# Row ends with places and loads of their own, splits behind the states and queries scaled on GpSimd, in a retention and expert kernel

## Chip, core and metric

One core of a Trainium2 chip (trn2). The metric is device time in microseconds (us) of one execution, from start to end; a kernel's time is the median of its runs, lower is better.

## What is computed

The reference chains three layers, all in float32. Only the first is touched here.

```python
# 1. retention: 4 batches, 8 heads, 576 positions, head size 64
scores = scale * q @ k.T
Dmat = where(rel >= 0, gamma[h] ** rel, 0)      # rel = pos_i - pos_j
ret = (scores * Dmat) @ v
# 2. dense layer on the 2304 tokens, 512 -> 2048 -> 512
h = x @ w_in;  x = (h * sigmoid(1.702 * h)) @ w_out
# 3. each token to one of 8 experts, 512 -> 1024 -> 512, scaled by its gate
out = gate_w * (relu(x @ w1[e]) @ w2[e])
```

## The kernel before

**Stages.** Attention (the retention) comes first, then the dense layer in six blocks of 384 tokens, then the experts. Each engine runs its own list of instructions in the order in which the program writes them; an engine that waits at one instruction holds back all behind it. Loads are issued by SP, also in order.

**Attention.** The work is cut into 16 rows (called `bp` in the code): a row is one batch and one pair of heads, four rows to a batch, so rows 0 to 3 are batch 0, 8 to 11 batch 2. A row's 576 positions are four chunks of 128 and an end of 64. Its chunks are 1 MB (`att`), loaded into one of eight buffers (`NBUF`); the buffer of row n is that of row n-8, and its load waits until that row's last use. The ends of a batch's four rows come in one load of 384 KB (`tails`). Two places hold them, so the ends of batches 2 and 3 take the places of batches 0 and 1 and are loaded when the last `ends_out` of those has run (line 417).

For a row, `decay` multiplies the keys by a table; `scores` makes k-by-q products of the four chunks in two PSUM banks; `masks` multiplies them by the table of decays on VectorE; `state` adds keys times values up chunk by chunk, and ScalarE copies each of the four partial sums out (line 324); `carried` multiplies the queries with these states; `chunk` adds the masked scores times values; `scores_end` and `ends_out` do the same for the ends. `keep` (VectorE) multiplies the result of 512 columns by the queries' decay and takes it out of PSUM, `keep_end` that of the end. For batches 0 and 1 `keep` then splits the result into a high part (ScalarE, line 378) and a low part (GpSimd, line 379) for the dense layer's first two blocks, or copies it (line 381); for batches 2 and 3 it goes straight to a buffer that is written to DRAM later.

The rows run in nine groups: [0], [1, 2], [3, 4] and so on to [13, 14], [15]; group k below is the k-th, from 0. In the loop over groups the current group's rows are `rows`, the next group's `nxt`, and the one after it `then`: `decay` of `then`, `scores_end` of `nxt`, `carried` and `ends_out` of `rows`, `scores` and `masks` of the first of `nxt`, and `values`, which alternates the states of `nxt` with the chunks of `rows`. Behind `values` the loads of rows bp+8 are issued; then come `scores` and `masks` of the second of `nxt`.

**Conversion beside it.** The dense weights come as 16 units of 64-bit words (`wd`, 1 MB each) that ScalarE and VectorE turn into float32 pairs (`convert`): for a unit the magnitude (ScalarE, line 166), two short VectorE steps (lines 179 and 181), two long ones (186, 193), the high part (ScalarE, 169) and the low part (VectorE, 173). `pull(us)` writes as many of these steps as its budget pays for at the place where it is called: in attention at each of the four `yield`s of a group from the third group on, with 0.5 us each. The first three units' loads go out at rows 8, 10 and 13 (`WD_AT`). A unit takes a buffer that attention has done with.

**Dense layer.** For blocks 0 and 1 the steps alternate over the units: `layer1` (12 matmuls into `h`), `swish` (ScalarE, then VectorE into `g..t`, ScalarE `g..h`, a `pull`, VectorE `g..l`), and two steps later `layer2` (9 matmuls into `o`), which needs `g..h` and `g..l`.

## Time and profile before

| | |
|---|---|
| runs, us | 742.16, 743.00, 743.25 (median 743.0) |
| the profiled execution's own time | 742.36 us |
| its span, first to last instruction | 740.6 us |
| TensorE busy | 707.4 us (96%) |
| VectorE, ScalarE, GpSimd busy | 456.2, 305.5, 195.3 us |
| mean granted TensorE clock | 0.988 |
| chain that ended last | TensorE 79%, DMA 13%, VectorE 3% |
| attention's matmuls | 5.7 to 95.8 us |

The profile is one execution, with times from its first instruction. "Busy" counts only the time in which an engine's instructions run; a wait is given with the work that ended it. TensorE (PE) is the busiest engine by far, but the share is a mean over the three stages, and the stage that is changed is the first 13% of the span.

### The profile page before, as it was taken

How to read it: one execution, taken by the hardware profiler on the slowest of the kernel's cores; microseconds unless marked ns; L12 is line 12 of the kernel's file. 1: busy time of each engine (PE TensorE's matmuls, PEld its weight loads, DVE VectorE, ACT ScalarE, POOL GpSimd, SP SyncE). 2: the span in 40 equal slices, each digit the busy share in tenths (PEclk: the TensorE clock that was granted, in tenths of full speed). 3: DMA queues.
4: the chain of work that ended last, by engine and by line, in shares of the span. 5: the costliest groups of instructions: out<-in, count | busy, mean ns of one | idle time of the engine just before them, and what ended most of it. 6: DMA issues, size and time to landing. Idle time of an engine off the chain costs nothing.

```text
span 740.6 us, 13083 instructions
## 1 busy us (share of the span) xinstructions
PE 707.4 (96%) x4882; PEld 654.6 (88%) x4882; DVE 456.2 (62%) x1045; ACT 305.5 (41%) x586; POOL 195.3 (26%) x186
## 2 busy tenths in 40 slices
PE   7875999999999999999999999999999999999995
PEld 6664789898999989899899898989999999999994
DVE  3553798988723887676367548747554654664661
ACT  3332444544427423332233233344345455455542
POOL 1632000000000023030102101224236456566563
PEclk9988999999999999999999999999999999999998
DMA  9955699900021004020210131152778789799861
GB/s 362 419 215 202 215 404 324 310 1 1 29 103 43 2 0 130 1 86 0 82 48 1 43 101 58 59 166 52 217 208 266 214 240 273 210 265 273 250 195 60
DMA packets 52579, 113.40 MB, mean 153 GB/s; under 512 B 8082, under 2 KB 28690, under 8 KB 48288
## 3 DMA queue, kind: packets, MB, share of 16 engines
q1 hardware_dynamic: 49168, 102.55, 43.4%
q0 software_dynamic: 3200, 9.46, 3.6%
q8 instruction: 39, 0.64, 0.3%
q10 hardware_dynamic: 144, 0.52, 0.2%
q14 instruction: 28, 0.23, 0.1%
HBM read 84.67 MB, written 28.17 MB: 152 GB/s over the span
## 4 chain that ended last, share of the span: by engine, by line
PE 79%; DMA 13%; DVE 3%; issue 3%; ACT 1%; POOL 1%; SPq 1%; POOLq 0%; ACTq 0%; DVEq 0%
PE o L501 27%; PE h L490 26%; PE eh L490 10%; PE eo L511 9%; DMA out<-y,idx 7%; DMA ends<-tails 4%; PE ao L332 1%; PE sc L292 1%; PE ao L349 1%; DMA we<-we 1%; PE s L323 1%; DMA row<-att 1%; PE tp L1007 1%; DVE ca L186 0%; DVE unit L173 0%
## 5 line engine op out<-in xcount | busy, mean ns | idle before, releaser
L490 PE MATMUL h<-x,unit 128*128 128x384 f32 x1152 | 217.6, 337 | 0.3 <-DVE g0t L523 0.3
L490 PEld LDWEIGHTS h<-x,unit 128*128 128x128 f32 x1152 | 204.6, 188 | 8.9 <-DVE g0t L523 0.6
L219 POOL TENSOR_TENSOR unit<-we,unit 128x512 fp32r<-128x512 f32 x64 | 102.5, 1609 | 118.2 <-ACT unit L217 107.1
L490 PE MATMUL eh<-xt,unit 128*128 128x336 f32 (+6 forms) x672 | 101.9, 300 | 0.0
L490 PEld LDWEIGHTS eh<-xt,unit 128*128 128x128 f32 x672 | 95.4, 188 | 0.4 <-ACT xt L731 0.2
L218 DVE TENSOR_TENSOR unit<-we,unit 128x512 fp32r<-128x512 f32 x64 | 56.3, 880 | 56.4 <-ACT unit L217 56.4
L597 DVE CUSTOM_DVE_ANT_0 dj<-xr,en 128x512 bf16<-128x512 f32 x120 | 78.0, 696 | 0.0
L217 ACT CAST unit<-we 128x1024 fp32r<-128x1024 f32 x64 | 66.8, 1046 | 23.0 <-DMA we<-we 21.3
L563 POOL TENSOR_TENSOR enrm<-scr,c 128x8 f32<-128x8 f32 x1 | 1.7, 1687 | 164.6 <-ACT ej L568 164.6
L324 ACT ACTIVATE ends<-s,tb 128x64 f32<-128x64 f32 x64 | 19.4, 312 | 47.2 <-PE s L323 46.5
L540 POOL DMA_INDIRECT out<-y,idx x24 | 24.8, 1032 | 30.1 <-ACT y L763 19.6
L540 POOL DMA_INDIRECT xs<-xr,slot x18 | 19.4, 1077 | 39.1 <-DVE xr L672 35.7
L323 PE MATMUL s<-row 128*64 128x64 f32 x256 | 20.2, 235 | 7.3 <-ACT ends L324 6.9
L323 PEld LDWEIGHTS s<-row 128*64 128x64 f32 x256 | 13.4, 135 | 13.6 <-ACT ends L324 12.2
L657 POOL TENSOR_TENSOR cum<-cum,oh_all 128x8 bf16<-128x8 bf16 x18 | 4.8, 265 | 67.2 <-PE rk L650 52.4
L314 POOL TENSOR_TENSOR row<-row,tb 128x512 f32<-128x512 f32 x14 | 14.5, 1044 | 28.5 <-DMA row<-att 28.5
L173 DVE TENSOR_TENSOR unit<-ca,unit 128x1024 fp32r<-128x1024 f32 x16 | 19.5, 1219 | 2.4 <-ACT unit L169 2.4
L292 PE MATMUL sc<-row 64*128 64x128 f32 x256 | 19.6, 294 | 0.8 <-DMA row<-att 0.8
L166 ACT ACTIVATE ca<-wd 128x1024 f32<-128x1024 f32 x16 | 18.4, 1147 | 4.8 <-DVE unit L173 4.8
L186 DVE SCALAR_TENSOR_TENSOR ca<-wd,ca 128x1024 int32<-128x1024 int32 x16 | 19.6, 1222 | 0.3
L193 DVE SCALAR_TENSOR_TENSOR ca<-wd,ca 128x1024 int32<-128x1024 int32 x16 | 19.5, 1217 | 0.0
L292 PEld LDWEIGHTS sc<-row 64*128 64x128 f32 x256 | 16.6, 197 | 2.9 <-issue 1.2
(1302 smaller groups left out, 1514.9 us busy)
## 6 DMA issues: line engine op xcount, KB each, us to landing
we<-we SPq DMA_DIRECT2D x64, 512.0 KB, 4.1
wd<-wd SPq DMA_DIRECT2D x16, 1024.0 KB, 11.9
row<-att SPq DMA_DIRECT2D x15, 1024.0 KB, 9.8
xs<-fill SPq DMA_DIRECT2D x22, 257.0 KB, 10.9
xrow<-xr SPq DMA_DIRECT2D x18, 257.0 KB, 4.0
y<-yd SPq DMA_DIRECT2D x7, 512.0 KB, 4.3
x0d<-x0f SPq DMA_DIRECT2D x4, 768.0 KB, 10.1
x0s<-x0d SPq DMA_DIRECT2D x8, 384.0 KB, 6.5
```

Of the source, the lines that this page charges most:

```text
L173: DVE.tensor_tensor(units[u][:, 1, :], word(u).bitcast(F32), units[u][:, 0, :].bitcast(F32), ALU.subtract)
L186: DVE.scalar_tensor_tensor(a, d[:, :, 1], -0x40000000, a, ALU.bitwise_and, ALU.bitwise_or)
L217: ACT.copy(w[:, 0, :], t)
L218: DVE.tensor_tensor(w[:, 1, :512], t[:, :512], w[:, 0, :512].bitcast(F32), ALU.subtract)
L219: POOL.tensor_tensor(w[:, 1, 512:], t[:, 512:], w[:, 0, 512:].bitcast(F32), ALU.subtract)
L292: PE.matmul(scs[j][:, P * ch : P * (ch + 1)], t[r, P * ch : P * (ch + 1)], t[r, AQ + P * ch : AQ + P * (ch + 1)], start=True, stop=True)
L323: PE.matmul(s[r], t[:, AK + c0 : AK + c0 + 64], t[:, AV + c0 : AV + c0 + 64], start=ch == 0, stop=True, skip_group_check=ch > 0)
L490: PE.matmul(h, w[:, a, P * dc : P * (dc + 1)], xt[:, b, dc, :n], start=k == 0, stop=k == len(terms) - 1)
L501: PE.matmul(o, a[:, c0 : c0 + n], w[:, b, 512:], start=first and k == 0, stop=last and k == 2)
L511: PE.matmul(o, w[:, b, D + P * d : D + P * (d + 1)], a, start=first and k == 0, stop=last and k == 2)
L540: i = POOL.indirect_dma_start(out=dst[:, :], out_offset=bass.IndirectOffsetOnAxis(ap=rows, axis=0), in_=src, in_offset=None, bounds_check= ...
L597: DVE.tensor_tensor_reduce(junk, r[:, :D], en[e // 4][:, e % 4, :], 1.0, 0.0, ALU.mult, ALU.add, dots[:, E * k + e : E * k + e + 1])
```

## The change

- **Ends.** A second buffer (`more`) gives each batch's ends a place of their own. They are loaded right in front of the batch's first row; the load at line 417 is gone. In exchange attention has six row buffers in place of eight (`NBUF`), and the loads of the first three weight units go out at rows 7, 9 and 11. Row 2 is loaded in two halves, keys and values first.
- **Order.** `scores_end` of the next group stands behind `ends_out` of this one.
- **Splits.** What `keep` did behind its multiplication is now `kept_out`, which stands behind all of `values`: ScalarE's splits and copies come after the eight states.
- **Queries.** For batches 2 and 3 GpSimd multiplies the queries by their decay when it decays the keys (128x512 each), and the queries of the ends of a batch (128x256) with its first row; ScalarE then copies the results out of PSUM, and VectorE has nothing to do in `keep` and `keep_end`. Row 1's keys are decayed by GpSimd, too.
- **Pulls.** Two `yield`s to a group, from group 3 on, with a budget of 0.8 us each in group 3 and 1.6 us after it.

```diff
-WD_AT = (8, 10, 13)
+WD_AT = (7, 9, 11)
-NBUF, NROW = 8, 6
+NBUF, NROW = 6, 5
...
-        ends = slot("ends")
-        tl = [ends[:, NPAIR * TAW * i : NPAIR * TAW * (i + 1)].rearrange("p (n w) -> p n w", w=TAW) for i in range(2)]
+        ends, more = slot("ends"), slot("more")
+        tl = [t[:, NPAIR * TAW * i : NPAIR * TAW * (i + 1)].rearrange("p (n w) -> p n w", w=TAW) for t in (ends, more) for i in range(2)]
...
         def load(bp):
             t = row[bp % NBUF]
-            if bp:
+            b, pair = divmod(bp, NPAIR)
+            if bp and pair == 0:
+                SP.dma_start(tl[b], tails[b])
+            if bp == 2:
+                SP.dma_start(t[:, AK:], att[bp, :, AK:])
+                SP.dma_start(t[:, :AK], att[bp, :, :AK])
+            elif bp:
                 SP.dma_start(t, att[bp])
...
-            if bp == 4:
-                SP.dma_start(tl[1], tails[1])
...
         def decay(bp):
...
-                (POOL if bp > 1 else DVE).tensor_tensor(kd, kd, dec.unsqueeze(2).to_broadcast(kd.shape), ALU.mult)
+                (POOL if bp else DVE).tensor_tensor(kd, kd, dec.unsqueeze(2).to_broadcast(kd.shape), ALU.mult)
+                b, pair = divmod(bp, NPAIR)
+                if b > 1:
+                    qd = row[bp % NBUF][:, AQ:AK].rearrange("p (c q) -> p c q", q=P)
+                    POOL.tensor_tensor(qd, qd, tbs[:, pair, :P].unsqueeze(1).to_broadcast(qd.shape), ALU.mult)
+                    if pair == 0:
+                        qe = tl[b][:, :, TQ:TV]
+                        POOL.tensor_tensor(qe, qe, tbs[:, :, :TAIL], ALU.mult)
...
         def keep_end(bp):
-            x = kept_in(bp)[:, NCH * P :]
-            DVE.tensor_tensor(x, st.pop(("ot", bp)), tbs[:, bp % NPAIR, :TAIL], ALU.mult)
+            x, o = kept_in(bp)[:, NCH * P :], st.pop(("ot", bp))
+            if bp // NPAIR > 1:
+                ACT.copy(x, o)
+            else:
+                DVE.tensor_tensor(x, o, tbs[:, bp % NPAIR, :TAIL], ALU.mult)
 
         def keep(bp):
+            if bp // NPAIR > 1:
+                return
...
+        def kept_out(bp):
             b, pair = divmod(bp, NPAIR)
...
             if b > 1:
+                ACT.copy(x[:, : NCH * P], o)
                 return
...
-            scores_end(nxt)
             for bp in rows:
                 carried(bp)
             ends_out(rows)
+            scores_end(nxt)
             for bp in rows:
                 keep_end(bp)
-                b, pair = divmod(bp, NPAIR)
-                if pair == NPAIR - 1 and b + 2 < B:
-                    SP.dma_start(tl[b], tails[b + 2])
-            yield
             if nxt:
                 scores(nxt[0])
                 masks(nxt[0])
-            yield
             values(rows, nxt)
             for bp in rows:
+                kept_out(bp)
...
-            yield
+            yield k
             for bp in nxt[1:]:
                 scores(bp)
                 masks(bp)
-            yield
+            yield k
...
-    for i, _ in enumerate(attention()):
-        if i >= 12:
+    for k in attention():
+        if k > 2:
             flush()
-            pull(0.5)
+            pull(0.8 if k == 3 else 1.6)
```

Three places show how the engines' lists move. A row of them gives the line, the operation, the tile written and those read (with the buffer's number) and the size; lines differ by some 4 to 16 between the two kernels. No time is in them.

SP's list from the fourth row's load on (`row5` is a row buffer, `ends` and `more` the ends' buffers, `wd0` a weight unit). Before:

```order
L258 DMA row4_84<-att 128x2048
L267 DMA ends_90<-tails 128x768
L258 DMA row5_85<-att 128x2048
L258 DMA row6_86<-att 128x2048
L258 DMA row7_87<-att 128x2048
L258 DMA row0_80<-att 128x2048
L136 DMA wd0_272<-wd 128x2048
L258 DMA row1_81<-att 128x2048
L258 DMA row2_82<-att 128x2048
L136 DMA wd1_383<-wd 128x2048
L417 DMA ends_90<-tails 128x768
```

and now:

```order
L259 DMA ends_88<-tails 128x768
L264 DMA row4_84<-att 128x2048
L264 DMA row5_85<-att 128x2048
L264 DMA row0_80<-att 128x2048
L264 DMA row1_81<-att 128x2048
L136 DMA wd0_374<-wd 128x2048
L259 DMA more_89<-tails 128x768
L264 DMA row2_82<-att 128x2048
L264 DMA row3_83<-att 128x2048
L136 DMA wd1_488<-wd 128x2048
```

The ends of batch 1 stand ahead of row 4 and those of batch 2 ahead of row 8 (now in `row2`); before, those of batch 2 stood behind row 10 (`row2`) and the second weight unit.

ScalarE in `values` of group 3, rows 5 and 6, with the states of rows 7 and 8 (`s7`, `s8`), the splits and copies of `x5` and `x6` and a magnitude (`ca`). Before:

```order
L324 ACTIVATE ends_90<-s7_554,tb_88 128x64
L324 ACTIVATE ends_90<-s8_560,tb_88 128x64
L378 CAST x0_1_96<-x5_535 128x192
L381 COPY x0f1_92<-x5_535 128x384
L324 ACTIVATE ends_90<-s7_554,tb_88 128x64
L324 ACTIVATE ends_90<-s8_560,tb_88 128x64
L324 ACTIVATE ends_90<-s7_554,tb_88 128x64
L324 ACTIVATE ends_90<-s8_560,tb_88 128x64
L378 CAST x0_1_96<-x6_537 128x192
L381 COPY x0f2_93<-x6_537 128x384
L166 ACTIVATE ca1_540<-wd1_383 128x1024
```

and now:

```order
L335 ACTIVATE ends_88<-s7_551,tb_86 128x64
L335 ACTIVATE ends_88<-s8_557,tb_86 128x64
L398 CAST x0_1_95<-x5_537 128x192
L401 COPY x0f1_91<-x5_537 128x384
L398 CAST x0_1_95<-x6_539 128x192
L401 COPY x0f2_92<-x6_539 128x384
L166 ACTIVATE ca0_606<-wd0_374 128x1024
L374 COPY x0f0_90<-at7_641 128x64
```

VectorE over the same rows: the first unit's short steps (`ca0`), masks (`sc0`, `sc1`) and `keep` (`x5`, `x6`). Before:

```order
L179 TENSOR_SCALAR ca0_539<-ca0_539 128x1024
L308 SCALAR_TENSOR_TENSOR pr_89<-sc0_102,tb_88 128x512
L308 SCALAR_TENSOR_TENSOR pr_89<-sc1_103,tb_88 128x512
L181 TENSOR_SCALAR ca0_539<-ca0_539 128x1024
L368 TENSOR_TENSOR x5_535<-ao5_512,tb_88 128x512
L368 TENSOR_TENSOR x6_537<-ao6_519,tb_88 128x512
L186 SCALAR_TENSOR_TENSOR ca0_539<-wd0_272,ca0_539 128x1024
L308 SCALAR_TENSOR_TENSOR tb_88<-sc0_102,tb_88 128x512
```

and now:

```order
L383 TENSOR_TENSOR x6_539<-ao6_515,tb_86 128x512
L179 TENSOR_SCALAR ca0_606<-ca0_606 128x1024
L181 TENSOR_SCALAR ca0_606<-ca0_606 128x1024
L312 SCALAR_TENSOR_TENSOR tb_86<-sc0_101,tb_86 128x512
L312 SCALAR_TENSOR_TENSOR tb_86<-sc1_102,tb_86 128x512
L186 SCALAR_TENSOR_TENSOR ca0_606<-wd0_374,ca0_606 128x1024
```

No split stands between two states any more; the first magnitude comes behind both rows' splits, and both short steps that need it stand ahead of the masks of row 8 (the last `sc0`, `sc1` of each list).

VectorE at the dense layer's start, from the end of attention to the first two results of `swish` (`g0t`, `g0l`). Before:

```order
L443 CAST ub_68<-uf_716 128x128
L193 SCALAR_TENSOR_TENSOR ca0_539<-wd2_605,ca0_539 128x1024
L179 TENSOR_SCALAR ca_1020<-ca_1020 128x1024
L523 SCALAR_TENSOR_TENSOR g0t_1054<-g0t_1054,h0_1041 128x384
L181 TENSOR_SCALAR ca_1020<-ca_1020 128x1024
L186 SCALAR_TENSOR_TENSOR ca_1020<-wd3_718,ca_1020 128x1024
L173 TENSOR_TENSOR unit2_1060<-ca0_539,unit2_1060 128x1024
L528 TENSOR_TENSOR g0l_1056<-g0t_1054,g0h_1055 128x384
```

and now:

```order
L181 TENSOR_SCALAR ca_1017<-ca_1017 128x1024
L186 SCALAR_TENSOR_TENSOR ca_1017<-wd3_827,ca_1017 128x1024
L173 TENSOR_TENSOR unit2_1023<-ca0_606,unit2_1023 128x1024
L193 SCALAR_TENSOR_TENSOR ca_1017<-wd3_827,ca_1017 128x1024
L459 CAST ub_68<-uf_825 128x128
L179 TENSOR_SCALAR ca_1017<-ca_1017 128x1024
L181 TENSOR_SCALAR ca_1017<-ca_1017 128x1024
L539 SCALAR_TENSOR_TENSOR g0t_1077<-g0t_1077,h0_1064 128x384
L186 SCALAR_TENSOR_TENSOR ca_1017<-wd4_844,ca_1017 128x1024
L173 TENSOR_TENSOR unit3_1057<-ca_1017,unit3_1057 128x1024
L193 SCALAR_TENSOR_TENSOR ca_1017<-wd4_844,ca_1017 128x1024
L544 TENSOR_TENSOR g0l_1079<-g0t_1077,g0h_1078 128x384
```

All of unit 3 (`wd3`) and the two short steps of unit 4 now stand ahead of `g0t`, and three long steps, not two and a short one, between `g0t` and `g0l`.

## Rows read from the trace of the kernel before

**Rows 1.** The page, granted TensorE clock in 40 slices of the span, in tenths.

```profile
PEclk9988999999999999999999999999999999999998
```

**Rows 2.** Stretches (us): length, busy PE, PEld, DVE, ACT, POOL, clock, DMA share, GB/s.

```profile
17.90:95.84 77.94, 59.39 (x1010) 51.09 (x1008) 43.83 (x82) 27.37 (x74) 21.85 (x26) 0.91 0.70 270
95.84:104.05 8.21, 7.05 (x40) 6.35 (x38) 8.18 (x12) 2.35 (x4) 0.00 (x0) 1.00 1.00 396
104.05:700.00 595.95, 595.29 (x3383) 554.54 (x3384) 382.43 (x916) 253.88 (x466) 151.64 (x137) 1.00 0.43 129
```

**Rows 3.** The chain of waits in time, attention: start us, us, what.

```profile
30.68 10.33 DMA ends<-tails
41.06 0.48 PE sct L298 x4
...
61.66 7.39 DMA ends<-tails
```

**Rows 4.** Waits in attention: engine, line, releaser: us in total, times, longest.

```profile
PE sct L298 <- DMA ends<-tails: 12.3, 3, 7.0
...
PE s L323 <- ACT ends L324: 6.9, 8, 1.7
```

**Rows 5.** Stretches of groups 5 and 6 without a wait, columns as in rows 2.

```profile
74.29:77.54 3.25, 3.25 (x66) 2.54 (x65) 2.10 (x3) 2.24 (x8) 0.00 (x0) 1.00 0.19 33
77.54:78.63 1.09, 1.09 (x18) 0.97 (x16) 0.97 (x2) 0.27 (x1) 0.00 (x0) 1.00 0.77 308
78.63:80.79 2.16, 2.16 (x51) 2.09 (x49) 2.16 (x4) 0.00 (x0) 0.00 (x0) 1.00 0.97 379
```

**Rows 6.** GpSimd's timeline: decays of rows 5 and 6 (start, us).

```profile
22.61 1.04 POOL L314 TENSOR_TENSOR row<-row,tb 128x512 f32<-128x512 f32 x1 [0.92 <-DMA row<-att]
25.09 1.04 POOL L314 TENSOR_TENSOR row<-row,tb 128x512 f32<-128x512 f32 x1 [1.44 <-DMA row<-att]
```

**Rows 7.** A stretch with loads queued; the last number is GB/s.

```profile
20.00:30.00 10.00, 8.91 (x168) 7.82 (x170) 4.88 (x10) 3.82 (x12) 6.34 (x9) 1.00 1.01 417
```

**Rows 8.** Views by line: operation, count, ns min/median/max; last, weight loads to landing.

```profile
L314 POOL TENSOR_TENSOR row<-row,tb x14: 1036/1044/1048, 12.8 to 71.7; 128x512 f32<-128x512 f32 x14
L314 DVE TENSOR_TENSOR row<-row,tb x2: 692/692/693, 6.1 to 10.3; 128x512 f32<-128x512 f32 x2
L219 POOL TENSOR_TENSOR unit<-we,unit x64: 1284/1788/1812, 443.6 to 717.4; 128x512 fp32r<-128x512 f32 x64
L308 DVE SCALAR_TENSOR_TENSOR pr<-sc,tb x22: 739/743/752, 6.9 to 91.4; 128x512 f32<-128x512 f32 x22
L378 ACT CAST x<-x x12: 345/351/511, 17.6 to 58.8; 128x192 fp32r<-128x192 f32 x8, 128x384 fp32r<-128x384 f32 x4
L166 ACT ACTIVATE ca<-wd x16: 1116/1148/1167, 37.7 to 189.5; 128x1024 f32<-128x1024 f32 x16
L179 DVE TENSOR_SCALAR ca<-ca x16: 680/686/695, 45.3 to 190.7; 128x1024 f32<-128x1024 f32 x16
DMA to landing us min/median/max: 4.7/11.9/15.2
```

**Rows 9.** VectorE's timeline at the dense layer's start.

```profile
99.98 0.54 DVE L523 SCALAR_TENSOR_TENSOR g0t<-g0t,h 128x384 f32<-128x384 f32 x1
...
101.17 1.23 DVE L186 SCALAR_TENSOR_TENSOR ca<-wd,ca 128x1024 int32<-128x1024 int32 x1
...
103.44 0.55 DVE L528 TENSOR_TENSOR g0l<-g0t,g0h 128x384 fp32r<-128x384 f32 x1
```

**Rows 10.** Waits of TensorE and what followed two of them, columns as in rows 2.

```profile
18.23:20.10 1.87, 0.00 (x0) 0.00 (x0) 1.18 (x2) 0.18 (x1) 0.95 (x1) 1.00 1.01 421
37.64:39.46 1.82, 0.00 (x0) 0.00 (x0) 1.18 (x2) 1.22 (x2) 1.82 (x3) 0.99 1.05 415
39.46:46.26 6.80, 5.20 (x56) 5.09 (x58) 1.43 (x5) 0.00 (x0) 0.62 (x1) 0.50 0.69 281
66.77:73.52 6.75, 4.43 (x50) 4.31 (x52) 0.96 (x5) 0.00 (x0) 2.68 (x4) 0.50 0.71 282
```

More of the change, by code (lines that the diff above doesn't have):

```diff
@@ L295, in scores_end @@
             for k, bp in enumerate(rows):
-                e = tl[bp // NPAIR % 2][:, bp % NPAIR, :]
+                e = tl[bp // NPAIR][:, bp % NPAIR, :]
                 for r in heads:
@@ L336, in ends_out @@
             for k, bp in enumerate(rows):
-                e, kv = tl[bp // NPAIR % 2][:, bp % NPAIR, :], kvs[bp % 2]
+                e, kv = tl[bp // NPAIR][:, bp % NPAIR, :], kvs[bp % 2]
                 o = st["ot", bp] = ot[:, TAIL * k : TAIL * (k + 1)]
@@ L360, in keep_end @@
         def keep_end(bp):
-            x = kept_in(bp)[:, NCH * P :]
-            DVE.tensor_tensor(x, st.pop(("ot", bp)), tbs[:, bp % NPAIR, :TAIL], ALU.mult)
-        def keep(bp):
+            x, o = kept_in(bp)[:, NCH * P :], st.pop(("ot", bp))
[3 more added lines that the diff above has]
+                DVE.tensor_tensor(x, o, tbs[:, bp % NPAIR, :TAIL], ALU.mult)
+        def keep(bp):
+            if bp // NPAIR > 1:
+                return
+            x, dec = kept_in(bp), tbs[:, bp % NPAIR, :P]
+            y, o = (a.rearrange("p (c q) -> p c q", q=P) for a in (x[:, : NCH * P], st["o", bp]))
+            DVE.tensor_tensor(y, o, dec.unsqueeze(1).to_broadcast(y.shape), ALU.mult)
+        def kept_out(bp):
             b, pair = divmod(bp, NPAIR)
-            x, dec = kept_in(bp), tbs[:, pair, :P]
-            y, o = (a.rearrange("p (c q) -> p c q", q=P) for a in (x[:, : NCH * P], st.pop(("o", bp))))
-            DVE.tensor_tensor(y, o, dec.unsqueeze(1).to_broadcast(y.shape), ALU.mult)
+            x, o = kept_in(bp), st.pop(("o", bp))
             if b > 1:
+                ACT.copy(x[:, : NCH * P], o)
                 return
```

## The prediction

> **What bounds the kernel now.** I read the page's slices first, to see where the clock falls: it is below full only in the first six of 40 slices and in the last [rows 1]. Then the stretches [rows 2]. In attention, from group 1's start at 17.90 to 95.84, TensorE is busy for 59.39 of 77.94 us at a mean clock of 0.91; from 104.05, the first full run of `layer2`, to 700 it is busy for 595.29 of 595.95. So behind 104.05 only TensorE's own work sets the time, and the change, which touches nothing there, is worth as much as it moves that point.
>
> What holds TensorE in attention stands in the chain and in the waits. The chain has two loads of row ends in it, 10.33 and 7.39 us long [rows 3]: TensorE reaches `scores_end`, waits, and all of the next group waits behind it. Three such waits make 12.3 us, the longest 7.0; eight waits for ScalarE's copies of the states make 6.9 [rows 4]. After the two long waits the granted clock is 0.50, which is 1.2 of 2.4 GHz, in two stretches in which TensorE is busy for 5.20 and 4.43 us [rows 10]; half of that is lost, 4.8 us. Idle time (77.94 - 59.39 = 18.55) and clock make 23.4 us, the most that a new order of attention can bring. A group without a wait takes 3.25 (`values`) + 1.09 (second `scores`) + 2.16 (`carried` and the ends) + 1.09 (first `scores`, the same form) = 7.6 us [rows 5].
>
> **The change, part by part.** I follow the new order from group 3 on, since up to there nothing waits long in it: ends 1 now land ahead of row 4.
>
> *Ends of batch 2.* They have a place, so no wait for `ends_out` is left, but they and row 8 stand behind the loads before them. GpSimd's decays of rows 5 and 6, which waited for their rows alone, begin 2.48 us apart [rows 6], which is one row of 1.05 MB at 417 GB/s [rows 7]. Up to row 6 the same bytes stand in SP's list as before, so I take its 25.09. Behind it come row 7, a weight unit, the ends (0.39 MB) and row 8: 3.54 MB, 8.5 us, so row 8 lands at 33.6. (With six buffers rows 7 and 8 wait for rows 1 and 2, but group 1's chunks are over by about 24, ahead of the transfer before.) Then GpSimd works on row 8: keys 1.04, queries and ends' queries before `scores_end` of group 4 may run. No row shows that scaling. Its bounds are 1.04 (the decays: same size, one operand repeated) and 1.81 (line 219's longest: two full operands) [rows 8]; I take line 219's shortest, 1.28, since here too both operands are read in full and VectorE's masks beside it have one operand in PSUM; half of it, 0.7, for the ends. So `scores_end` runs at 33.6 + 1.04 + 1.28 + 0.7 = 36.6. TensorE would be there at about 34.7: group 1's start near 17.6, two groups of 7.6, and 1.9 of `carried` and `ends_out`; it waits 1.9.
>
> The row says that GpSimd takes 1.04 us where VectorE takes 0.69 for the same operation, 1.5 times as long [rows 8]. The Trainium skill (GPSIMD Engine Reference, 4.1 Engine selection) speaks against this move: it gives elementwise work with two inputs to VectorE because GpSimd needs about twice its time. By that the two scalings would take 1.4 and 0.7, and the sum would be 0.1 later.
>
> The rate of 417 GB/s is that of a stretch with loads queued throughout [rows 7]. The Trainium skill (DMA: Bandwidth & Descriptors, Where 436 GB/s comes from) lets the HBM side, about 358 GB/s for a core, bind such loads. By that the 8.5 us would be 9.9 and row 8 would land 1.4 later; the trace's rate is higher and decides.
>
> *Group 3's end.* From 36.6: the rest of `scores_end` and `scores` 1.2, `values` 3.25 (to T = 41.1), second `scores` 1.09, so group 4 begins at 42.2.
>
> *The first conversion steps.* At T ScalarE turns to the splits and copies of rows 5 and 6, four of some 0.35 and 0.51, 1.7 together, then to the magnitude, 1.15; VectorE's two short steps behind it take 0.69 each; only then come row 8's masks, 0.74 each, 1.4 for both [rows 8]. They end at T + 5.7. TensorE wants the banks for its next `scores` at T + 1.09 + 2.16 = T + 3.25: a new wait of 2.5 us. It may be nothing if the steps were done ahead of row 8's scores, but the list has them behind. In later groups the steps fall into `values`, where VectorE no longer has `keep` to do, and cost nothing.
>
> *Groups 4 to 8.* 3 x 7.6, then 6.5 for group 7, which has one row to follow and so no second `scores`, and 2.1 for the single row 15 (1.1 for half of `carried` and the ends, four chunks of 0.25): 31.4. This takes the waits for ScalarE as gone, since no split stands between two states. ScalarE's new copies of 512 columns, 0.62 by line 378's 0.35 at 192 and 0.51 at 384, hide behind the second `scores`; if they don't, each group loses what they are late, at most 1 us. GpSimd's scalings, some 2.6 a group, lie beside TensorE's 7.6. Ends 3 and row 12 land near 50 and are wanted near 55. `keep` and `keep_end` leave VectorE, which was waiting anyway: nothing. Attention ends at 42.2 + 2.5 + 31.4 = 76.1, where it was 95.84.
>
> *The dense layer's start* gives some back. Let V be the end of group 7's `values`, 76.1 - 2.1 = 74.0. ScalarE has a last copy (0.6) and unit 3's magnitude (1.15), to V + 1.8. VectorE then has unit 3's four steps, a low part and two steps of unit 4 ahead of `g0t`: four short ones at 0.69, three long ones at 1.22 and a cast of 0.2, 6.6 [rows 8, 9]; `g0t` 0.54 is done at V + 9.0, then three long ones and `g0l`, 4.2: V + 13.2, 11.1 behind attention's end. Before, `layer2` ran 8.2 behind it. So 2.9 goes back, in two waits of some 2.8 and 1.9 where there were shorter ones. Unit 3's load is issued at the end of group 6's `values`, V - 7.4, and lands in 4.7 at best [rows 8], 3.3 ahead of its magnitude: hidden, unless it takes over 8 us. `layer2` is reached at 76.1 + 11.1 = 87.2, 16.9 us earlier than 104.05.
>
> *The clock.* After 1.87 us of idling TensorE kept its clock; another time it lost it 1.82 us into a wait, and 5.20 busy us followed at half, a loss of 2.6, or 2.2 in the second case [rows 10]. The new order has waits of 1.9, 2.5 and 2.8, all between the case that kept the clock and the waits that lost it. I count one drop, 2.4; none and two are the bounds.
>
> *Sum.* -16.9 + 2.4 = -14.5 on the profiled execution's 742.36: 727.9. The median shown is 743.0, 0.6 above that execution, which I leave out. I forecast **728**.
>
> **Rivals.** *Quicker:* the clock stays up (-2.4) and the wait for row 8's masks is short (-2.5), so 723; if VectorE also gives nothing back at the dense start (-2.9), 720. For it: each of the waits is near the one that kept the clock. Against: three such waits.
>
> *The weights come late:* unit 3 or 4 lands with the 11.9 us that is the median for such loads [rows 8] instead of 4.7 to 8, and `g0t` and `g0l` are 4 us later: 732; with a second drop 734. For it: their buffers are freed only by rows 12 and 13. Against: attention's loads are over by then, so the queue is short.
>
> *Slower than before:* six buffers starve the groups. A buffer is free in the middle of one group's `values` and its next row must be loaded, decayed and scaled before the first `scores` two groups on, 2 x 7.6 - 1.6 - 1.1 = 12.5 us, less GpSimd's 2.3: 10.2 for the load. Each us beyond that is lost in each of groups 4 to 7. To eat 14.5 us, loads of 13.8 us would be needed in all four, and 18 us would give 728 + 31 = 759. For it: loads took 10.3 and 7.4 even for 0.39 MB in a full queue [rows 3]. Against: with six buffers at most two rows, a unit and the ends are in flight, 3.5 MB or 8.5 us.
>
> *No gain:* ends 2 and 3 have their places, but the queue, not the place, was what they waited for, and group 3 and group 5 still wait as long: then only the waits for ScalarE fall away, 742.4 - 6.9 + 2.9 = 738, and with a drop and a late VectorE, no change.
>
> **How the numbers follow.** Forecast case, 724 to 732: 0.55. Quicker, 719 to 724: 0.25. Late weights, 731 to 735: 0.10. No gain, 0.07: 0.05 of it still faster, 0.02 no change. Slower: 0.03. The range takes the first three: 719 at the low end; at the high end 728 with a second drop (2.4), the longest scaling (0.8), and one more load of 1 MB ahead of row 8 (2.5), 734, so 735 with the late weights. Three runs lie within 742.16 to 743.25, so 0.2%, 1.5 us, is about what can be told from no change. Faster 0.95, same 0.02, slower 0.03.
>
> **What would show it.** Right: no wait of TensorE for a load of ends at `scores_end`, but one of about 2 us for GpSimd in group 3; a wait of about 2.5 us for row 8's masks at the start of group 4; groups 5 and 6 of 7.6 us; attention's end near 76 and `layer2` near 87; the rest as before. Wrong: waits for rows' loads in groups 4 to 7, or a `layer2` that begins later than 92.

## The result, and the profile after

The changed kernel takes **732.05 us** (median of 4 runs, 730.68 to 733.67) against 743.12 of the kernel before on the same chip: a ratio of 0.985, with a 95% interval of 0.982 to 0.988. The forecast was 728.0 in a range of 719 to 735: direction and range hold, and the middle was 4 us too low. The profiled execution took 732.19 us, its span is 730.2.

| us | before | forecast | after |
|---|---|---|---|
| group 4 begins | | 42.2 | 45.48 |
| attention ends | 95.84 | 76.1 (78.5 with the clock's 2.4) | 81.44 |
| first full run of `layer2` | 104.05 | 87.2 (89.6) | 91.95 |
| from there to the end of the span | 636.55 | as before | 638.25 |

TensorE's waits after the change (engine, line, releaser: us in total, times, longest), which answer to [rows 4]; L302 is now `scores_end`, L334 `state`, L296 `scores`, L506 and L517 the dense layer:

```profile
PE sct L302 <- POOL more L325: 2.8, 1, 2.8
PE h L506 <- DVE g0t L539: 2.2, 1, 2.2
PE sc L296 <- issue: 1.6, 1, 1.6
PE s L334 <- POOL row L318: 1.4, 2, 0.8
PE o L517 <- DVE g0l L544: 1.3, 1, 1.3
...
PE s L334 <- ACT ends L335: 0.8, 3, 0.3
PE ao L343 <- ACT x0f L389: 0.7, 1, 0.7
```

No load of ends is in it any more (12.3 us before), the waits for ScalarE's copies of the states fell from 6.9 to 0.8, and the wait of 2.8 is for GpSimd (L325, the scaling of the ends' queries). Two waits for GpSimd's decays of keys, 1.4 us together, stand in groups 0 and 1; before the change there were none. The stretches, columns as in [rows 2]: groups 3 to 8, the dense layer's start, and two pieces of groups 3 and 4:

```profile
33.54:45.48 11.94, 9.12 (x146) 8.20 (x145) 4.93 (x10) 3.86 (x13) 9.51 (x11) 0.86 0.77 297
45.48:56.72 11.24, 9.53 (x147) 8.35 (x145) 7.69 (x12) 5.11 (x15) 5.82 (x5) 0.85 0.80 319
56.72:64.48 7.76, 7.76 (x146) 6.63 (x144) 7.63 (x10) 5.88 (x15) 7.54 (x8) 1.00 0.81 273
64.48:72.32 7.84, 7.84 (x147) 6.81 (x145) 7.14 (x10) 4.88 (x14) 6.09 (x5) 1.00 0.28 105
72.32:79.38 7.06, 6.22 (x111) 5.07 (x109) 6.41 (x8) 3.20 (x10) 0.00 (x0) 1.00 0.62 196
...
81.44:91.95 10.51, 7.04 (x40) 6.35 (x38) 10.25 (x14) 4.35 (x8) 0.00 (x0) 1.00 0.94 368
...
39.60:43.02 3.42, 3.42 (x44) 3.20 (x42) 1.56 (x3) 1.26 (x4) 3.13 (x4) 0.50 0.45 189
49.84:53.26 3.42, 3.39 (x32) 3.17 (x34) 3.14 (x6) 0.69 (x3) 2.21 (x2) 0.50 0.93 384
```

Groups 5 and 6 take the 7.6 us of a group without a wait, within 0.25. What is still lost lies in groups 3 and 4 (11.94 and 11.24): one stop each, and behind each 3.42 us at clock 0.50, which is 1.2 of 2.4 GHz, so at most 1.7 us lost each time. (The run with the wait filled, below, does the same work of group 3 at full clock in 5.43 us, from 38.98 to 44.41, where the changed kernel takes 6.74, from 38.74 to 45.48: 1.3 us.) The view puts the stop in group 4 (1.55 us, then 0.16) down to "issue". VectorE's timeline shows what it ends with, the first of row 8's two masks, behind the conversion's short steps:

```profile
47.80 0.69 DVE L181 TENSOR_SCALAR ca<-ca 128x1024 int32<-128x1024 int32 x1
48.41 1.40 DVE L312 SCALAR_TENSOR_TENSOR tb<-sc,tb 128x512 f32<-128x512 f32 x2
```

GpSimd's timeline shows what the first wait is made of (start, us):

```profile
35.52 1.04 POOL L318 TENSOR_TENSOR row<-row,tb 128x512 f32<-128x512 f32 x1 [4.40 <-DMA row<-att]
36.52 1.26 POOL L322 TENSOR_TENSOR row<-row,tb 128x512 f32<-128x512 f32 x1
37.74 0.69 POOL L325 TENSOR_TENSOR more<-more,tb 128x256 f32<-128x256 f32 x1
```

Row 8 landed at 35.5, 1.9 later than forecast, and `scores_end` waits for the third of three steps. The loads' rate shows where some two thirds of that were lost (GpSimd's busy time, clock, DMA share; the last number is GB/s):

```profile
22.00:23.00 1.00, 1.00 (x2) 1.00 0.99 401
23.00:24.00 1.00, 0.72 (x2) 1.00 0.52 213
24.00:25.00 1.00, 0.72 (x1) 1.00 0.77 172
25.00:26.00 1.00, 0.00 (x0) 1.00 0.75 311
26.00:27.00 1.00, 0.95 (x1) 1.00 0.99 418
```

From 23 to 26 the queue ran dry. With six buffers row 7's load waits until TensorE has read the last of row 1, at 23.3; it is issued at 23.4, when what stood ahead of it had been moved, and the rate is back at its level only at 26. At 417 GB/s [rows 7] three slices would move 1251 and moved 696 (both in GB/s x us): an estimate of 1.3 us.

### The profile page after: what moved, and what is told of

Same layout as the page of the kernel before. It is cut to its first block, busy times and chain, and to the rows that moved or that the text cites. A ratio compares the mean times of both kernels' runs of the same rounds, so it can differ in the third digit from the quotient of the medians.

```text
span 730.2 us, 13107 instructions
## 1 busy us (share of the span) xinstructions
PE 706.4 (97%) x4882; PEld 653.7 (90%) x4882; DVE 451.7 (62%) x1028; ACT 311.4 (43%) x602; POOL 212.8 (29%) x197
## 5 line engine op out<-in xcount | busy, mean ns | idle before, releaser
L506 PE MATMUL h<-x,unit 128*128 128x384 f32 x1152 | 217.6, 337 | 2.2 <-DVE g0t L539 2.2
L506 PEld LDWEIGHTS h<-x,unit 128*128 128x128 f32 x1152 | 204.6, 188 | 10.8 <-DVE g0t L539 2.5
L506 PE MATMUL eh<-xt,unit 128*128 128x336 f32 (+6 forms) x672 | 102.2, 301 | 0.5 <-DVE eg54l L551 0.5
L506 PEld LDWEIGHTS eh<-xt,unit 128*128 128x128 f32 x672 | 95.5, 188 | 1.1 <-DVE eg54l L551 0.7
L318 POOL TENSOR_TENSOR row<-row,tb 128x512 f32<-128x512 f32 x15 | 18.7, 1250 | 29.4 <-DMA row<-att 18.1
L334 PE MATMUL s<-row 128*64 128x64 f32 x256 | 21.1, 245 | 2.6 <-POOL row L318 1.4
L296 PE MATMUL sc<-row 64*128 64x128 f32 x256 | 20.4, 295 | 2.6 <-issue 1.6
L334 PEld LDWEIGHTS s<-row 128*64 128x64 f32 x256 | 14.9, 145 | 8.4 <-ACT ends L335 5.2
L173 DVE TENSOR_TENSOR unit<-ca,unit 128x1024 fp32r<-128x1024 f32 x16 | 20.3, 1271 | 1.6 <-ACT unit L169 1.6
L296 PEld LDWEIGHTS sc<-row 64*128 64x128 f32 x256 | 16.9, 195 | 4.9 <-issue 2.9
L479 POOL TENSOR_TENSOR x<-x0s,x 128x768 fp32r<-128x768 f32 x3 | 6.1, 2029 | 48.6 <-ACT x L478 48.6
```

Of the source, the lines that this page charges most:

```text
L173: DVE.tensor_tensor(units[u][:, 1, :], word(u).bitcast(F32), units[u][:, 0, :].bitcast(F32), ALU.subtract)
L296: PE.matmul(scs[j][:, P * ch : P * (ch + 1)], t[r, P * ch : P * (ch + 1)], t[r, AQ + P * ch : AQ + P * (ch + 1)], start=True, stop=True)
L334: PE.matmul(s[r], t[:, AK + c0 : AK + c0 + 64], t[:, AV + c0 : AV + c0 + 64], start=ch == 0, stop=True, skip_group_check=ch > 0)
L506: PE.matmul(h, w[:, a, P * dc : P * (dc + 1)], xt[:, b, dc, :n], start=k == 0, stop=k == len(terms) - 1)
```

## The experiments

All times beside the kernel before on the same chip. "Wait" is that of `scores_end` in group 3, "masks" the wait for row 8's masks in group 4, "half" the number of stretches at clock 0.50 in attention and at the dense layer's start. What stands right of the ratio is from one profiled execution of each. The mean granted clock differs between executions of one kernel (0.992 to 0.997 over the five of "ends' queries first"), so the number of stretches is that execution's and need not be the same in the next.

| kernel | us | ratio (95%) | wait | masks | half | attention ends | `layer2` |
|---|---|---|---|---|---|---|---|
| changed kernel | 732.05 | 0.985 (0.982 to 0.988) | 2.83 | 1.7 | 2 + 0 | 81.4 | 91.95 |
| ends' queries first | 728.18 | 0.981 (0.980 to 0.983) | 0 | 1.7 | 0 | 77.0 | 87.53 |
| unit 0 behind row 8 | 729.18 | 0.983 (0.982 to 0.985) | 0.80 | 2.4 | 1 + 1 | 79.3 | 89.83 |
| masks first | 732.49 | 0.986 (0.984 to 0.988) | 2.86 | 0 | 2 + 0 | 86.1 | 95.21 |
| ends and masks first | 725.04 | 0.977 (0.976 to 0.979) | 0 | 0 | 0 | 75.9 | 84.98 |
| the same, unit 0 ahead of row 7 | 724.74 | 0.976 (0.974 to 0.978) | 0 | 0 | 0 | 76.3 | 85.45 |
| the same, conversion earlier | 725.88 | 0.977 (0.975 to 0.979) | 0 | 0 | 0 | 75.3 | 85.79 |
| wait filled with products | 732.10 | 0.986 (0.984 to 0.988) | 1.34 | 2.7 | 1 + 1 | 81.5 | 91.97 |
| splits inside `values` | 732.34 | 0.986 (0.984 to 0.988) | 0.69 | 1.7 | 0 + 1 | 81.9 | 92.45 |
| splits inside, ends and masks first | 727.97 | 0.981 (0.979 to 0.983) | 0 | 0 | 0 | 79.8 | 88.88 |
| queries on VectorE | 730.26 | 0.984 (0.982 to 0.987) | 0 | 1.7 | 0 + 1 | 76.5 | 89.06 |
| places shared | 747.52 | 1.006 (1.004 to 1.008) | see text | | 2 + 0 | | |
| places shared, scaled behind the load | 729.85 | 0.984 (0.981 to 0.987) | 1.75 | 1.7 | 1 + 1 | 79.5 | 90.09 |

### What holds `scores_end` in group 3

**Ends' queries first.**

```diff
+                if b > 1 and pair == 0:
+                    qe = tl[b][:, :, TQ:TV]
+                    POOL.tensor_tensor(qe, qe, tbs[:, :, :TAIL], ALU.mult)
                 (POOL if bp else DVE).tensor_tensor(kd, kd, ...)
                 if b > 1:
                     POOL.tensor_tensor(qd, qd, ...)
-                    if pair == 0:
-                        qe = tl[b][:, :, TQ:TV]
-                        POOL.tensor_tensor(qe, qe, tbs[:, :, :TAIL], ALU.mult)
```

> The changed kernel, with GpSimd scaling the ends' queries of a batch before the keys and queries of its first row, not behind them. Theory (scores_end in group 3 waits for GpSimd's order of work: 1.04 + 1.26 us of row 8's own work stand ahead of the 0.69 it needs, and that work waits for row 8's landing at 35.5, while the ends land before row 8): the scaling is done by 35.3, the wait of 2.83 us at scores_end is gone, at most 0.5 us shows up at row 8's first state instead, the clock stays up, group 4 starts near 41.3 instead of 45.48, and the time is about 4 us under 732, near 728. Rival 1 (the ends land together with row 8, since transfers in the queue share the engines): the scaling cannot begin before 35.5 and ends at 36.2, the wait is 0.6 us at scores_end and 0.7 more at row 8's states, time 729.5. Rival 2 (VectorE's conversion sets the dense layer's start): group 4 early, layer2 at 91.95 as now, 732.

Its GpSimd timeline (L321 is the ends' scaling, L322 the keys), and TensorE's wait for row 8's masks in group 4:

```profile
33.05 0.68 POOL L321 TENSOR_TENSOR more<-more,tb 128x256 f32<-128x256 f32 x1 [2.06 <-DMA more<-tails]
35.62 1.04 POOL L322 TENSOR_TENSOR row<-row,tb 128x512 f32<-128x512 f32 x1 [1.89 <-DMA row<-att]
...
44.83 0.46 PE L296 MATMUL sc<-row 64*128 64x128 f32 x2 [1.56 <-issue]
```

The ends had landed at 33.05, 2.5 us ahead of row 8. The wait is gone, no stretch at half clock is left, `layer2` begins 4.42 earlier and the time is 728.18, as the theory had it (3.9 us under the changed kernel, 2.7 by the ratios). So the wait of 2.83 us was GpSimd's order of work, not the load of what `scores_end` needs. It also took the second stretch at half clock, which I had not expected: the wait for row 8's masks is as long as before (1.56 us here), but the clock now survives it. Little of that arrives: group 4 takes 10.68 and not 11.24, since a wait of 0.77 for ScalarE's copies is new in it.

**Unit 0 behind row 8.** `WD_AT = (8, 9, 11)` for `(7, 9, 11)`.

> The changed kernel with weight unit 0 loaded behind row 8 instead of ahead of it. Theory (row 8 lands late because 1 MB more stands ahead of it, and the wait of 2.83 us at scores_end in group 3 and the half clock behind it come from that): row 8 lands 2.5 us earlier, near 33.0, GpSimd is done with it near 36.0, the wait falls to under 0.5 us, the clock stays up there, group 4 starts near 41.6 instead of 45.48, and the time is 3 to 4 us under the changed kernel's 732, near 728.5. Rival 1 (the transfers set nothing, GpSimd's own queue does): the wait stays over 2 us, 732. Rival 2 (VectorE's conversion sets where the dense layer starts, and unit 0 now comes late): group 4 starts early but layer2 does not move from 91.95, 732.

TensorE in groups 3 and 4:

```profile
36.65 0.33 PE L302 MATMUL sct<-more 64*64 64x64 f32 x4 [0.80 <-POOL more L325]
...
46.84 0.46 PE L296 MATMUL sc<-row 64*128 64x128 f32 x2 [2.27 <-issue]
```

The first wait shrinks to 0.80 and group 4 begins at 42.35. Part of it comes back at once, in a longer wait for the masks and a stretch at half clock behind that; 729.18. Row 8's keys begin 1.84 earlier, at 33.68, but the ends' scaling still stands third, so the gain is less than with the ends first.

**Unit 0 ahead of row 7, unit 2 behind row 12**, with ends and masks first: `WD_AT = (6, 9, 12)`.

> The version with the ends' queries first and no conversion steps ahead of row 8's masks, and with weight unit 0 loaded behind row 6, ahead of row 7, and unit 2 behind row 12 instead of row 11. Theory (row 8 landed 1.9 us later than forecast in good part because the queue ran dry between 23 and 26, 213, 172 and 311 GB/s where it has 417: row 7's load waits for the buffer of row 1, and a unit with a place of its own can fill that gap; and row 12 waits behind unit 2): GpSimd begins row 8's keys at 34.0 to 34.5 instead of 35.5, the wait of 1.13 us for row 12's keys in group 5 goes, layer2 begins near 84.0, time 724. Rival (both were hidden, or what they give is taken back by VectorE's conversion at the dense layer's start): layer2 at 85, 725.

The loads' rate in the same slices (the last number), and GpSimd at row 8:

```profile
23.00:24.00 1.00, 1.00 0.97 401
24.00:25.00 1.00, 1.00 1.04 434
25.00:26.00 1.00, 1.00 1.05 434
```

```profile
31.93 0.69 POOL L321 TENSOR_TENSOR more<-more,tb 128x256 f32<-128x256 f32 x1
...
34.37 1.04 POOL L322 TENSOR_TENSOR row<-row,tb 128x512 f32<-128x512 f32 x1 [1.75 <-DMA row<-att]
...
46.55 0.34 PE L334 MATMUL s<-row 128*64 128x64 f32 x4 [1.25 <-ACT ends L335]
```

The gap is filled and row 8's keys begin at 34.37 instead of 35.52: 1.15 us of the late landing were the dry queue. The time is that of the version without it (724.74 against 725.04, overlapping intervals): the rival's number. In the trace the wait of 1.13 for row 12's keys is gone, as the theory had it, but a wait of 1.25 for ScalarE's copies (the last line) is new in group 4, and attention ends no earlier (76.3 against 75.9).

### The masks of row 8, and VectorE

**Masks first.**

```diff
+    first = False
     for k in attention():
-        if k > 2:
+        if k > 2 and (k > 3 or first):
             flush()
             pull(0.8 if k == 3 else 1.6)
+        first = k == 3
```

> The changed kernel, with no conversion steps ahead of row 8's masks in group 3 (they begin behind them). Theory (the wait for row 8's masks at the start of group 4, 1.55 + 0.16 us, comes from the magnitude and the two short steps ahead of them, and the second stretch at half clock comes from that wait): both go, group 4 takes 7.8 us instead of 11.24, so attention ends near 78; the conversion is two short steps (1.4 us) later, which the dense layer's start takes back, so layer2 begins 1.5 to 2.5 us earlier than 91.95 and the time is near 730. Rival 1 (VectorE's conversion is the only thing that sets the dense layer's start): attention ends 3.4 us earlier, layer2 not at all, 732. Rival 2 (the clock falls in group 4 anyway, as a late echo of the wait in group 3): group 4 takes about 9.5 us, 731.

TensorE at `scores_end` of groups 3 and 5:

```profile
38.74 0.48 PE L302 MATMUL sct<-more 64*64 64x64 f32 x4 [2.86 <-POOL more L325]
...
60.45 0.48 PE L302 MATMUL sct<-more 64*64 64x64 f32 x4 [3.80 <-POOL more L325]
```

The wait for the masks is gone, and none of it arrives in time (732.49, the number of rival 1, though for another reason): TensorE comes to group 5's `scores_end` earlier and waits 3.80 us for the same kind of scaling, behind row 12 (its keys begin at 56.41, once it lands). None of the three expectations had that. The profiled execution is the slowest of the four, 734.72: its stretch at half clock in group 3, ahead of anything the edit moves, is 6.35 us long (38.17 to 44.52) and not 3.42. So its 86.1 and 95.21 in the table are later than the edit made them.

**Ends and masks first**: both edits.

> Both: ends' queries scaled first, and no conversion steps ahead of row 8's masks. Theory (the two waits are separate and each brings its own stretch at half clock): the gains add, no stretch of attention behind 20 us has the clock at 0.50, group 3 and group 4 take 7.7 us each, attention ends near 73.5, and layer2 begins 5 to 6 us earlier than 91.95; time near 726. Rival (VectorE's conversion has become the bound, so only what starts the conversion earlier counts): the same time as the one with the ends' queries first alone, near 728, with the waits for g0t and g0l longer by what attention gained.

From group 3's start to attention's end (columns as in [rows 2]):

```profile
33.39:75.85 42.46, 39.59 (x722) 33.43 (x720) 34.04 (x50) 24.39 (x65) 27.23 (x26) 1.00 0.75 289
```

The clock is full throughout, and with 725.04 this version **beats both kernels**: 2.3% under the one before, 0.8% under the changed one by the ratios. Of the 2.55 us that `layer2` gains over the ends first alone, attention gives 1.16; the rest is about a long step of the conversion (1.22), which stood ahead of `g0l` in VectorE's list and now stands behind it. Attention ends at 75.85 and not near 73.5: groups 5 and 7 take 8.94 and 8.30, 1.2 more each than in the changed kernel, with a wait of 1.13 for row 12's keys in group 5.

**Conversion earlier**: as the version with unit 0 ahead of row 7, but the first steps stand ahead of group 3 (`if k > 2 and len(seen) != 7 or len(seen) == 6`, where `seen` counts the yields).

> As the one before, and the conversion begins ahead of group 3, in VectorE's idle time of some 3 us there, instead of at its end. Theory (with the waits of attention gone, VectorE's conversion sets the dense layer's start, where TensorE still waits 1.2 and 0.9 us for g0t and g0l): those two waits lose 1.4 to 2 us, layer2 begins near 82.5, time 722 to 723. Rival 1 (unit 0 lands too late for that, and VectorE in its order holds up row 7's masks behind it): a new wait of 1 to 2 us in group 3, 725 or more. Rival 2 (VectorE and GpSimd slow each other where both work, so steps moved beside GpSimd's scaling of row 8 save nothing): 724.

VectorE's first two steps, beside GpSimd's scaling of row 8 (L325, from 35.55 to 37.27):

```profile
35.36 0.78 DVE L179 TENSOR_SCALAR ca<-ca 128x1024 f32<-128x1024 f32 x1
36.17 1.64 DVE L181 TENSOR_SCALAR ca<-ca 128x1024 int32<-128x1024 int32 x1
```

Attention ends 1 us earlier, `layer2` does not (85.79 against 85.45): in VectorE's list that long step stands ahead of `g0l` again, and TensorE waits 2.2 and 1.3 us for `g0t` and `g0l` as in the changed kernel. Rival 2 is seen too: the second step takes 1.64 instead of 0.69.

### The clock

**Wait filled with products** of the ones, ahead of row 8's part of `scores_end`; they go to a part of a bank that nothing reads.

```diff
             for k, bp in enumerate(rows):
+                if bp == 8:
+                    for _ in range(26):
+                        PE.matmul(sct[:64, 256:384], ones[:, :64], ones, start=True, stop=True)
```

> The changed kernel with 26 products of the ones (bf16, into a part of a bank that nothing reads) ahead of the one matmul of scores_end in group 3 that waits for GpSimd, some 2.7 us of work by the 0.105 us of such a product at the kernel's start, so that TensorE works through most of the wait. Theory (the stretch at clock 0.50 from 39.8 to 42.9 follows from TensorE having nothing to do in that wait): the wait itself stays as long as it was, the clock stays at 1.00 there, group 4 starts about 1.5 us earlier than 45.48, the second stretch at half clock, behind the masks, stays; time 730.5. Rival 1 (the clock falls at that time whatever TensorE does): as now, 732. Rival 2 (the products hold TensorE longer than the wait): group 4 starts at 45 to 46, 732.

TensorE's two waits, and the work of group 3 between them; then VectorE and GpSimd ahead of the second:

```profile
38.72 0.33 PE L305 MATMUL sct<-more 64*64 64x64 f32 x4 [1.34 <-POOL more L328]
38.98 1.16 PE L296 MATMUL sc<-row 64*128 64x128 f32 x16
...
44.41 1.53 PE L346 MATMUL ao<-row,ends 64*64 64x128 f32 x24
...
49.22 0.46 PE L296 MATMUL sc<-row 64*128 64x128 f32 x2 [2.58 <-issue]
```

```profile
46.01 1.00 DVE L179 TENSOR_SCALAR ca<-ca 128x1024 f32<-128x1024 f32 x1 [1.88 <-ACT ca L166]
47.04 1.42 DVE L181 TENSOR_SCALAR ca<-ca 128x1024 int32<-128x1024 int32 x1
48.38 1.40 DVE L315 SCALAR_TENSOR_TENSOR tb<-sc,tb 128x512 f32<-128x512 f32 x2
```

```profile
46.73 1.18 POOL L321 TENSOR_TENSOR row<-row,tb 128x512 f32<-128x512 f32 x1 [0.27 <-PE sct L305]
47.87 1.54 POOL L325 TENSOR_TENSOR row<-row,tb 128x512 f32<-128x512 f32 x1
```

The products took 1.64 us of the wait, not the expected 2.7. The scaling ended as late as ever, the clock stayed at 1.00 through group 3, and group 4 began at 44.41, 1.07 earlier: the first stretch at half clock did follow from TensorE's idleness, as far as one execution of each kernel shows it. The gain was lost in the next group: row 8's masks are ready at the same 49.2, since VectorE's two short steps, now beside GpSimd's work on row 11, took 2.4 us instead of 1.4, and the wait of 2.58 us brought its own stretch at half clock.

### Which part of the change brought the time

**Splits inside `values`**, where they stood before the change (batches 0 and 1; the same lines out of the loop behind `values`).

```diff
                 if ch == NCH - 1:
                     keep(bp)
+                    if bp // NPAIR < 2:
+                        kept_out(bp)
```

> The changed kernel with ScalarE's splits and copies of the rows of batches 0 and 1 back inside values, right behind each row's product, as they stood before the change. Theory (TensorE's eight waits for ScalarE's copies of the states, 6.9 us before the change, came from these splits, and all belong to groups with such rows): the waits come back, 4 to 7 us over groups 0 to 4, layer2 begins near 96 to 98 instead of 91.95, and the time is 736 to 739. Rival 1 (what the splits take is hidden, since these groups wait for loads and GpSimd anyway): within 1 us of 732. Rival 2 (the longer groups let row 8 land ahead of scores_end, so the wait of 2.83 us and a stretch at half clock go): 733.

```profile
PE s L334 <- ACT ends L335: 5.5, 8, 1.0
...
PE sct L302 <- POOL more L325: 0.7, 1, 0.7
```

The eight waits are back (5.5 us; the fence shows TensorE's waits as above), and the wait at `scores_end` falls by 2.1 and attention has no stretch at half clock; with one at the dense layer's start it is 732.34. Rival 2. **The same with ends and masks first:**

> The version with the ends' queries first and no conversion steps ahead of row 8's masks (725.0), with ScalarE's splits back inside values. In the changed kernel itself this cost nothing: 5.5 us of waits for ScalarE came back, and the wait for GpSimd at scores_end fell by 2.1, with its half clock. Theory (that was a substitution: the splits' place is worth its waits once nothing else holds these groups): 4 to 5.5 us of waits for ScalarE come back and show in full, layer2 begins at 88 to 90 instead of 84.98, time 729 to 730. Rival (the waits for ScalarE are taken back elsewhere, by VectorE's conversion having more time before the dense layer's start): 726 to 727.

Seven waits for ScalarE, 4.9 us in all; `layer2` 3.9 us and the time 2.9 us later than without them (727.97 against 725.04), between the two expectations. So the splits' new place was worth nothing in the changed kernel, as GpSimd's wait stood behind it, and 3 us once that wait is gone.

**Queries on VectorE**: the scaling by GpSimd out, `keep` and `keep_end` as before the change.

> The changed kernel with GpSimd's scaling of queries and ends' queries of batches 2 and 3 left out, and their outputs scaled by VectorE behind the product, as before the change. Theory (the scaling on GpSimd costs at scores_end in group 3 and is repaid by VectorE's time for the conversion): the wait of 2.83 us and its half clock go, so group 4 starts near 41.2 instead of 45.48; VectorE has some 0.69 x 8 + 0.2 x 8 = 7 us more in groups 4 to 8, the conversion is late by 3 to 6 us at the dense layer's start, with waits for g0t and g0l together of 6 to 9 us instead of 3.5; time 731 to 734. Rival 1 (VectorE's slack in attention takes the 7 us): layer2 near 87.5, time 728, and the scaling on GpSimd is a loss. Rival 2 (the scaling is the main gain): 736 and more.

Attention ends 5 us earlier than in the changed kernel; the dense layer's first wait, for `g0t`, is 4.28 us instead of 2.18, and `layer2` gains 2.9. The time of 730.26 lies between the theory's and rival 1's, and the interval does not tell it from the changed kernel. With its ends first, the scaling on GpSimd looks the better of the two (728.18; 0.981 against 0.984, the intervals touch).

**Places shared**: `tl = [tl[0], tl[1], tl[0], tl[1]]`, and `tails[b + 2]` loaded behind `ends_out` of a batch's last pair.

> The changed kernel with the ends of batches 2 and 3 loaded into the places of batches 0 and 1, behind the last ends_out that reads these, as before the change; all else (six buffers, weight units, scaling) stays. Theory A (the place of their own is what took the long waits for ends away): the load can only be issued once group 2's ends_out is over, near 29, takes 7 to 10 us as before the change, and scores_end in group 3 waits for a load again: 3 to 5 us more than now, time 735 to 738. Theory B (with six buffers the queue ahead of the ends is short, so the same load at the same point lands by 36 to 37, hardly later than row 8's own work on GpSimd; the place does little): the wait at scores_end in group 3 stays at 2.5 to 4 us, group 5 waits for nothing, time 732 to 733.

The edit left GpSimd's scaling ahead of the load, so it worked on the ends' queries of batches 0 and 1 while those of 2 and 3 stayed unscaled, and `ends_out` of group 2 waited 10.07 us for it, which is the landing of row 8. That is another question, so the next run moves the scaling behind the load too.

> As the run with the places shared, but GpSimd scales the ends' queries of batches 2 and 3 behind their load, which is what that run was to compare. Theory A (the place of its own is what took the long waits for ends away): the load, issued once group 2's ends_out is over, near 29, waits for TensorE and then takes 7 to 10 us, so scores_end in group 3 waits until 40 or later instead of 38.48; 3 to 5 us more, 735 to 738. Theory B (with six buffers instead of eight the queue ahead of the ends is short, and the same load at the same point lands by 36 to 37, while row 8, with 0.39 MB less ahead of it, lands at 34.6): the wait at scores_end in group 3 is 2 to 4 us, in group 5 none, time 731 to 733, and the place alone is worth nothing.

The issue of the ends' load, their scaling (L437), and TensorE's wait for it:

```profile
27.76 0.33 SPq L435 DMA_DIRECT2D ends<-tails  x1
...
36.67 0.68 POOL L437 TENSOR_TENSOR ends<-ends,tb 128x256 f32<-128x256 f32 x1
...
37.41 0.33 PE L303 MATMUL sct<-ends 64*64 64x64 f32 x4 [1.75 <-POOL ends L437]
```

Theory B. Without a place of their own the ends are scaled by 37.35, ahead of the changed kernel's 38.43: row 8 no longer stands behind them in the queue of loads, and its keys begin at 34.45 and not at 35.52. The time is not above the changed kernel's.

## Why the prediction came out as it did

- **What bounds the kernel, and that TensorE alone does behind `layer2`**: held. The span is 10.4 us shorter; `layer2` came 12.1 earlier, and 1.7 was given back behind it (0.9 more idle time, of it 0.78 a wait for `g1l`, and 0.8 more busy time). "The rest as before" was 1.7 off.
- **"Row 8 lands at 33.6"** failed by 1.9: the step that cost most. It took a queue that never runs dry, since "group 1's chunks are over by about 24, ahead of the transfer before". Row 1's were over at 23.3, but that is not ahead of the transfers: nothing else was left to move then. The run with unit 0 ahead of row 7 gives 1.15 of it back. Some 0.7 (an estimate by 417 GB/s) lies between 10 and 12, where the rate was 266 GB/s, so the same bytes up to row 6 did not bring the same times either: row 5's keys begin 1.07 later than before (23.68 against 22.61). The queue was not dry there (DMA share 0.91), and row 2's load, now in two halves, was landing (its keys begin at 12.49); whether the halves cost that, no run tests. The rate itself was right: 385 to 443 GB/s in every slice from 26 to 35. By the estimate from the Trainium skill (DMA: Bandwidth & Descriptors, Where 436 GB/s comes from) row 8 would have landed 1.4 later, near the 35.5 measured; the agreement is chance, as the slices show a gap and no lower rate.
- **GpSimd's prices**, 1.28 and 0.7: measured 1.09 to 1.30 where VectorE was not in the way, and 0.69. The estimate from the Trainium skill (GPSIMD Engine Reference, 4.1 Engine selection) was 1.4; the trace stays below that there, and goes to 2.07 where both engines work.
- **The wait at `scores_end`**, 1.9: 2.83. `scores_end` ran at 38.48, 1.9 later than forecast, which is the late landing, and TensorE itself came 0.95 later, at 35.65, of it 0.55 a wait for GpSimd's decay of row 4 in group 1, where the text had "nothing waits long". I took GpSimd's order as given; the run with the ends first shows the wait as a matter of that order alone.
- **The masks**, 2.5 us: 1.55 + 0.16. The chain was right: group 3's `values` ended at 45.48 - 1.09 = 44.4, and the masks were done at 49.8, 5.4 later, where 5.7 stood in the sum. But the next `scores` needs only the first bank, so one mask of 0.74 was counted too many: 0.8 less than forecast.
- **One drop of the clock**, 2.4: two, each of 3.42 us at half clock. By the comparison above one cost 1.3, so two some 2.6: the number of drops was wrong and the sum near by luck.
- **Groups 5 to 7**, 21.7: 22.66, of it 0.73 for ScalarE's copy of 512 columns in group 7, which the text had as "at most 1 us".
- **The dense layer's start**, 11.1 with waits of 2.8 and 1.9: 10.51, with 2.18 and 1.29.
- Together, along the time axis: group 4 begins 3.3 later than forecast and takes 1.1 more than 7.6 + 2.5, groups 5 to 7 take 1.0 more, the dense layer's start 0.6 less, and 1.7 comes behind it: 6.5. Less the 2.4 that the sum held for the clock, that is the 4.1 us between the span's forecast and measured gain.
- **The reason for the gain** was partly wrong though the sum was near. The ends' own places, told first, are worth nothing in the changed kernel: that rival ("the queue, not the place") was right about the mechanism and wrong about the time, since the ends' load also comes in time without a place. (With the ends scaled first it was not tried: TensorE then wants them at 35.4, and in the run with shared places they were scaled only by 37.35.) The splits' place and GpSimd's scaling are worth nothing alone either, each being covered by another wait. What remains is the order of loads with six buffers, the new place of `scores_end` behind `ends_out`, and that of the pulls; none of these was undone alone. For the loads speaks that in the run with shared places the ends were loaded and scaled 9.6 us after their issue at 27.76, where before the issue came at 30.68 and the load alone took 10.33 [rows 3]. Eight buffers with all else of the change were not tried, so what the larger part of the gain comes from is argued and not shown.

## What to carry to other kernels

Where one engine prepares several things for a waiting one, put what is waited for first in its list, by when each input lands: that single move was worth 4.4 us at the dense layer's start here, over a third of what the whole change moved it. When a part of a change is undone and nothing moves, look for the wait that grew or shrank in its place before calling the part useless; it shows its price once that wait is gone. A smaller ring of buffers seems to shorten the queue ahead of urgent loads (argued, not shown), but look for the moment when nothing is queued, and put a transfer with a place of its own there: here it brought the next row 1.15 us earlier, though no time.

## What the runs showed of the hardware

**VectorE and GpSimd hold each other up.** VectorE's step L181 takes 0.69 us alone, and 1.42 and 1.64 beside GpSimd's scalings (fences above); GpSimd's scaling takes 1.09 to 1.30 alone and up to 2.07 in the changed kernel. There, between 62 and 66, one VectorE step of 1.22 took 2.06 while GpSimd's decay and scaling took 1.77, not 1.04, and 2.07:

```profile
63.45 2.06 DVE L173 TENSOR_TENSOR unit<-ca,unit 128x1024 fp32r<-128x1024 f32 x1
...
64.39 2.07 POOL L322 TENSOR_TENSOR row<-row,tb 128x512 f32<-128x512 f32 x1
```

The masks, with one operand in PSUM, stay at 1.40 for two. The Trainium skill (SBUF — State Buffer, Who interferes with whom) says that GpSimd shares a port pair of SBUF with VectorE, and that VectorE's instructions with two SBUF inputs or in a two-port mode contend for it while others don't. The trace agrees for L173, which reads two tiles in SBUF, and for the masks; that L181, with one, runs in a two-port mode, no run here shows. So moving work to GpSimd has a price on VectorE that the sum did not hold.

**The length of a wait alone does not tell whether the clock falls.** TensorE's wait for `g0t` of 2.18 to 2.22 us was followed by a stretch at 0.50 in four kernels (unit 0 behind row 8, the filled wait, splits inside `values`, places shared with the scaling behind the load) and by none in four (the changed kernel, ends first, conversion earlier, places shared). In attention it fell behind one wait of 1.75 us and every one from 2.27 up, and not behind 1.34 and four of 1.51 to 1.56; but before the change 1.87 kept it [rows 10], and in the changed kernel 1.55, for the masks, lost it. Each of these is one execution. What decides between 1.5 and 2.2 us stays open; a sum can only carry it as a range.
